# Two-scale attention and a token-choosing MLP on one core: loads in rows of 4,608 B, ranking scores transposed and counted whole, and another table of places

## The chip, the cores and the metric

The kernel runs on one core of one Trainium2 chip. The metric is the device time of one execution in microseconds; before the change the median of three runs is 291.59 us (290.5 to 292.26).

## What is computed

Inputs are q, k and v of 8 batches, 8 heads, 576 tokens and 64 numbers, and the weights of a small MLP. The reference, cut to what matters:

```python
# per batch and head; sm_attn is softmax attention
q_d, k_d, v_d = means of q, k, v over 4 neighbouring tokens      # 144 coarse tokens
out_up    = np.repeat(sm_attn(q_d, k_d, v_d), 4, axis=2)
mask      = abs(pos[:, None] - pos[None, :]) < 4                 # a band of 7 keys
out_local = softmax(where(mask, scale * q @ k.T, -1e9)) @ v
x         = (out_up + out_local) as [batch, 576, 512]
# per batch
scores  = x @ w_gate
top_idx = the 128 tokens with the highest score
h       = maximum(x[top_idx] @ w1, 0)                            # w1: 512 x 1024
out     = x;  out[top_idx] += sigmoid(scores[top_idx])[:, None] * (h @ w2)
```

## The kernel before

The host lays the inputs out, and the kernel works through eight batches in overlapping stages. For each batch b:

- **load** (`load_qk`, `load_v`): q and k of two heads share the 128 partitions; the tile T holds, per partition, four head pairs of q and k with 576 tokens each, 18,432 B. Batch 0 comes in four loads of one head pair (4,608 B a partition), every other batch in one. `raw` holds v by its four places within a coarse token, 9,216 B a partition. `vw` holds v in windows of 64 keys, in three loads. There are two buffers T and one `raw`.
- **sums** (`pool_qk`, `load_v.add`): the means over four tokens, as sums into dT and vd, by GpSimd (for batch 0 those of q and k by VectorE). `half` is the step between.
- **coarse**: scores of the coarse tokens on TensorE (line 527, with 534 for the tokens over 128), maximum on VectorE, exponentials on ScalarE, transposes (511, 589 to 591), products with vd (601 to 623), division on VectorE into ods and odr.
- **lift**: the coarse rows are repeated four times into x, for batches 0 and 1 by matmuls (`raise_by_products`, 676 to 692, with one GpSimd step `apart`, 664), for the others by DMA copies within SBUF (`raise_by_copies`).
- **local**: banded attention in five tiles of 116 queries: mask and scores (754, 766), maximum and difference (777, 778), exponential (786), transposes (511), products (812), division (822 to 824), the sum into x (834: VectorE for batches 0 and 7, GpSimd for the rest) and the dot product with the gate (841). Then x is stored to DRAM.
- **route**: the 128 highest of 576 scores. The scores stand as 5 columns of 128 in `scp`. `rows` transposes each column, spread over 128 columns, so that every partition sees all scores (895). `compare` (908) then sets on VectorE, for tile j, where a score of tile j or later is beaten, and sums that up for tile j; `count` (919) adds on TensorE what the later tiles lost in these comparisons. `rank` joins the two, `hot` makes one-hot columns, `pick` (946) turns them into token numbers, and `gather` fetches the tokens' rows of x from DRAM.
- **moe**: `turn` (984) transposes the 128 rows, eight `up` blocks (1005 to 1007, 12 matmuls each) and eight `down` blocks (1027 to 1029, three each) are the MLP with f16 weights in high and low parts, `join` (1035) multiplies by the gate and `scatter` writes the rows back.

Each stage is cut into steps, 934 in all, each of one engine. A planner keeps lists of what is ready and hands out buffers; which ready step comes next is told by PLACES, a table of 934 numbers, one for each step, the lowest first. The instructions of each engine then stand in that order and wait in that order. All loads and stores but the gather and scatter are issued by SP, which also issues in order. The wait for a buffer, for instance the one `raw`, holds up what SP issues behind it.

In the names of the rows, `ps` is PSUM, `hid` is also the buffer in which the f32 weights land, `xe` that of the gate at the start, and `cst` the constants, which come in two loads (lines 360 and 386).

Of the kernel before, what the change touches and what calls it, by code (L numbers as in the profile page):

```python
# [11 lines left out]
F32 = mybir.dt.float32  # L12
F16 = mybir.dt.float16
BF16 = mybir.dt.bfloat16
# [66 lines left out]
"""  # L81


class Buf:


    def __init__(self, tag, line=None):
        self.tag, self.line, self.at, self.left = tag, line or tag, None, 0
        self.banks = {"pair": 2, "bank": 1}.get(tag, 0)

# [1049 lines left out]
```

## Time and profile before

| | |
|---|---|
| median of three runs | 291.59 us |
| lowest and highest | 290.5 and 292.26 us |
| the profiled execution's own time | 292.61 us |
| its span | 290.8 us |
| mean granted TensorE clock | 0.962 of full speed |
| busy: TensorE matmuls | 233.5 us (80%) |
| busy: VectorE | 216.1 us (74%) |
| busy: GpSimd | 162.8 us (56%) |
| busy: ScalarE | 127.3 us (44%) |

The profile is of one execution, and its times are of that one. A busy share is a mean over stages with different limits; the table by stage and the lists of waits say more on which engine sets the pace where. "Idle before, releaser" names what ended the wait of an instruction; "issue" stands where the trace shows nothing that the engine waited for. PE is TensorE, PEld its weight loads, DVE VectorE, ACT ScalarE, POOL GpSimd, SPq the queue of SP.

### The profile page before, as it was taken

The page shows a single profiled execution, that of the slowest core. Times are in us where ns is not written, and L with a number is a line of the kernel's source. Part 1 is how long each engine was busy: PE and PEld are TensorE (multiplying, and loading weights), DVE is VectorE, ACT ScalarE, POOL GpSimd, SP SyncE. Part 2 cuts the span into 40 slices and gives each one's busy share as a digit, 9 for nine tenths or more (in the row PEclk, how much of TensorE's full clock was granted, in tenths as well). Part 3 has the DMA queues.
Part 4 walks back from the last instruction along what each step waited for, and adds up shares of the span by engine and source line. Part 5 has one row for each costly group of instructions (what it writes and reads, how often), then busy time and mean ns, then how long its engine had stood idle before and what let it go on. Part 6 is the DMA issues. An engine that isn't in the chain of part 4 may idle for free.

```text
span 290.8 us, 12080 instructions
## 1 busy us (share of the span) xinstructions
PE 233.5 (80%) x5280; PEld 171.6 (59%) x5280; DVE 216.1 (74%) x507; ACT 127.3 (44%) x264; POOL 162.8 (56%) x177
## 2 busy tenths in 40 slices
PE   1776966498677677997789989899999899789892
PEld 0654553366446556755676658756885775657570
DVE  5986497986996969977968799688988888632121
ACT  0476475348573445256605544365333233041010
POOL 8248878369876858939696976943613302202011
PEclk9999799969999957999999999999999999999998
DMA  7999978666798999868997598786887703502000
GB/s 273 423 412 389 407 280 327 241 149 177 238 341 292 315 341 377 257 197 261 347 278 223 174 325 270 194 214 140 205 240 187 182 17 103 135 2 72 2 36 36
DMA packets 19518, 66.01 MB, mean 227 GB/s; under 512 B 3346, under 2 KB 3346, under 8 KB 17546
## 3 DMA queue, kind: packets, MB, share of 16 engines
q1 hardware_dynamic: 18186, 61.06, 64.9%
q0 software_dynamic: 1280, 4.20, 4.4%
q8 instruction: 41, 0.67, 0.9%
q14 instruction: 11, 0.09, 0.1%
HBM read 47.02 MB, written 11.73 MB: 202 GB/s over the span
## 4 chain that ended last, share of the span: by engine, by line
PE 51%; issue 14%; DVE 13%; DMA 8%; ACT 6%; SPq 3%; POOL 1%; POOLq 0%; DVEq 0%
PE ps L766 5%; PE ps L1005 5%; PE ps L812 5%; PE ps L511 4%; PE ps L1027 4%; DMA out_dram<-x 4%; PE ps L1007 4%; PE ps L1006 4%; PE ps L1029 3%; PE ps L1028 3%; PE ps L527 2%; DMA T<-in_qk_dram 2%; PE ps L609 2%; DMA hid<-in_moe_w_dram 2%; DVE t L841 2%
## 5 line engine op out<-in xcount | busy, mean ns | idle before, releaser
L834 POOL TENSOR_TENSOR x<-x,t 128x512 f32<-128x512 f32 x30 | 39.3, 1320 | 21.1 <-DVE t L824 13.3
L1005 PE MATMUL ps<-xeh,w1h 128*128 128x128 f16 x256 | 45.2, 220 | 3.5 <-DVE hid L1017 1.7
L1007 PE MATMUL ps<-xeh,w1l 128*128 128x128 f16 x256 | 45.0, 219 | 0.0
L1006 PE MATMUL ps<-xel,w1h 128*128 128x128 f16 x256 | 45.0, 219 | 0.0
L766 PE MATMUL ps<-T 64*58 64x64 f32 (+1 forms) x1280 | 28.3, 230 | 6.6 <-issue 6.5
L777 DVE TENSOR_REDUCE mx<-ps 128x16 f32<-128x1024 f32 (+1 forms) x24 | 25.0, 1042 | 10.5 <-PE ps L766 10.5
L812 PE MATMUL ps<-vw,pt 64*64 64x65 f32 x1280 | 28.1, 226 | 5.4 <-ACT ed L559 1.5
L766 PEld LDWEIGHTS ps<-T 64*58 64x58 f32 (+1 forms) x1280 | 26.9, 139 | 9.1 <-issue 8.2
L841 DVE SCALAR_TENSOR_TENSOR t<-x,ps 128x512 f32<-128x512 f32 x40 | 26.9, 684 | 7.0 <-PE ps L1007 3.9
L490 POOL TENSOR_TENSOR half<-T 128x1152 f32<-128x1152 f32 x14 | 29.5, 2106 | 3.9 <-DMA T<-in_qk_dram 3.6
L812 PEld LDWEIGHTS ps<-vw,pt 64*64 64x64 f32 x1280 | 22.9, 136 | 13.6 <-issue 4.2
L798 ACT COPY pt<-ps 128x1024 f32<-128x1024 f32 (+1 forms) x24 | 20.8, 872 | 19.3 <-PE ps L511 19.3
L824 DVE TENSOR_TENSOR t<-ps,den 128x512 f32<-128x512 f32 x40 | 27.7, 691 | 1.5
L1014 ACT ACTIVATE hid<-ps 128x512 f16<-128x512 f32 x16 | 9.6, 597 | 43.7 <-PE ps L1007 21.2
L1006 PEld LDWEIGHTS <-w1h 128*128 128x128 f16 x256 | 25.0, 98 | 4.9 <-issue 4.1
L786 ACT ACTIVATE ex<-ex 128x1024 f32<-128x1024 f32 (+1 forms) x24 | 22.0, 916 | 13.3 <-DVE ex L778 11.9
L1027 PE MATMUL ps<-w2h,hid 128*128 128x512 f16 x64 | 24.3, 380 | 4.0 <-DVE hid L1017 1.3
L527 PE MATMUL ps<-dT 64*64 64x144 f32 x256 | 14.8, 337 | 15.3 <-DVE dT L482 7.2
L961 POOL DMA_INDIRECT xe<-out_dram,idx x8 | 8.4, 1045 | 33.4 <-DVE gs L956 22.3
L1005 PEld LDWEIGHTS <-w1h 128*128 128x128 f16 x256 | 25.0, 98 | 1.7
L778 DVE TENSOR_TENSOR ex<-ps,mx 128x1024 f32<-128x1024 f32 (+1 forms) x24 | 25.1, 1047 | 0.8
L1007 PEld LDWEIGHTS <-w1l 128*128 128x128 f16 x256 | 25.0, 98 | 0.0
(113 smaller groups left out, 533.3 us busy)
## 6 DMA issues: line engine op xcount, KB each, us to landing
T<-in_qk_dram SPq DMA_DIRECT2D x7, 2304.0 KB
raw<-in_vp_dram SPq DMA_DIRECT2D x8, 1152.0 KB
vw<-in_vw_dram SPq DMA_DIRECT2D x16, 520.0 KB
out_dram<-x SPq DMA_DIRECT2D x14, 480.0 KB
x<-ods SPq DMA_DIRECT2D x48, 120.0 KB
hid<-in_moe_w_dram SPq DMA_DIRECT2D x8, 512.0 KB
T<-in_qk_dram SPq DMA_DIRECT2D x4, 576.0 KB
vw<-in_vw_dram SPq DMA_DIRECT2D x8, 260.0 KB
```

The costliest lines, as they stand in the source:

```text
L490: pool.tensor_tensor(out=hv.at, in0=e2[..., 0], in1=e2[..., 1], op=ALU.add)
L766: pe.matmul(s.at[64 * e : 64 * e + qn, a, c : c + KW], lhsT=T.at[64 * a : 64 * a + 64, hp, 0, q0s[blk] : q0s[blk] + qn], rhs=T.at[64 * a : ...
L777: dve.tensor_reduce(out=mx.at[:, :, :ng], in_=sv, axis=AX.X, op=ALU.max)
L778: dve.tensor_tensor(out=ex.at[:, :ng, :].rearrange("p g (a c) -> p a g c", a=2), in0=sv, in1=mx.at[:, :, :ng].unsqueeze(3).broadcast_to([P ...
L812: pe.matmul(o.at[64 * e : 64 * e + 64, a, D1 * hp : D1 * (hp + 1)], lhsT=pt.at[64 * a : 64 * a + 64, e, HP * n + hp, :], rhs=vl.at[64 * a ...
L824: dve.tensor_tensor(out=t.at.rearrange("p (g a d) -> p a g d", a=2, d=D), in0=ov[:, :, :, 0:D], in1=den.at.unsqueeze(3).broadcast_to([P, 2 ...
L834: (dve if last else pool).tensor_tensor(out=x.at[:, j], in0=x.at[:, j], in1=t.at, op=ALU.add)
L841: dve.scalar_tensor_tensor(out=t.at, in0=x.at[:, j], scalar=1.0, in1=wg, op0=ALU.mult, op1=ALU.mult, accum_out=sc.at[:, j : j + 1],)
L1005: pe.matmul(o, lhsT=w1h[:, c, fs], rhs=xeh.at[:, c, :], start=c == 0, stop=False)
L1006: pe.matmul(o, lhsT=w1h[:, c, fs], rhs=xel.at[:, c, :], start=False, stop=False)
L1007: pe.matmul(o, lhsT=w1l[:, c, fs], rhs=xeh.at[:, c, :], start=False, stop=c == NC - 1)
L1027: pe.matmul(py.at, lhsT=hid.at[:, 0, f, :], rhs=w2h[:, f, :], start=f == 0, stop=False)
```

## The change

It has three parts. First, the host lays q and k out with the head pair outermost, and v in two halves by place, so that a load that had one row of 18,432 B (q and k) or 9,216 B (v) for a partition now has four or two rows of 4,608 B for it; the tiles in SBUF and the number of loads stay. Second, `rows` transposes each column of scores in one piece of 128 partitions in place of two of 64, so that the rows stand one after the other, and `count` counts a tile's 128 tokens with one matmul in place of two; `compare` sees the same numbers in another layout. Third, PLACES has other numbers, so that the order of the steps changes on every engine. The planner's cost of `rows` goes from 390 to 550.

```diff
 PLACES = """
-    0 1 10 23 18 68 73 2 3 4 5 6 25 32 8 9 7 12 67 75 15 62 208 79 112 151 156 193 211 214 238 249 221 245 253 267 288
+    0 1 10 12 18 49 50 2 3 4 5 6 25 33 7 8 9 11 37 46 15 52 59 51 88 173 63 98 185 177 207 248 190 231 244 256 287 317
...
-    B, _, HP, _, S = qk.shape
+    B, HP, _, _, S = qk.shape
...
-    first = cpool.tile([P, 2, NT, 64], F32, name="first")
+    first = cpool.tile([P, NT * P], F32, name="first")
...
-    slots("beat", 3, [P, 2, NT, 64], BF16)
+    slots("beat", 3, [P, NT, P], BF16)
...
-                sp.dma_start(out=T.at[:, n * u : n * (u + 1)], in_=qk[b][:, n * u : n * (u + 1)])
+                sp.dma_start(out=T.at[:, n * u : n * (u + 1)], in_=qk[b, n * u : n * (u + 1)].rearrange("h p n s -> p h n s"))
...
-            "SP", 0, lambda: sp.dma_start(out=raw.at, in_=vp[b]), (), (raw,), pref("load", b, 0.35),
+            "SP", 0, lambda: sp.dma_start(
+            out=raw.at.rearrange("p (r s) h d -> p r (s h d)", r=2), in_=vp[b].rearrange("r p s h d -> p r (s h d)"),
+        ), (), (raw,), pref("load", b, 0.35),
...
+            sbf = sb.at.rearrange("p a (j u) -> p (a j) u", u=P)
             for j in range(NT):
-                for e in range(2):
-                    lo, hi = 64 * e, 64 * e + 64
-                    pe.transpose(
-                        sb.at[:, e, 64 * j : 64 * j + 64], scp.at[lo:hi, j : j + 1].broadcast_to([64, P]),
-                        ident[lo:hi, lo:hi],
-                    )
+                pe.transpose(sbf[:, j], scp.at[:, j : j + 1].broadcast_to([P, P]), ident)
...
-        step("PE", 390, rows, (scp, "cst", "cbf"), (sb, q), pr, 170)
+        step("PE", 550, rows, (scp, "cst", "cbf"), (sb, q), pr, 170)
...
                 for k in range(j + 1, NT):
-                    for e in range(2):
-                        pe.matmul(
-                            q.at[64 * e : 64 * e + 64, k : k + 1], lhsT=beat.at[:, e, k - j], rhs=ones, start=False,
-                            stop=j == NT - 2, skip_group_check=True,
-                        )
+                    pe.matmul(
+                        q.at[:, k : k + 1], lhsT=beat.at[:, k - j], rhs=ones, start=False,
+                        stop=j == NT - 2, skip_group_check=True,
+                    )
...
-    qk = np.stack([q, k]).reshape(2, B, hp, 2, S, D).transpose(1, 3, 5, 2, 0, 4)
-    qk = np.ascontiguousarray(qk).reshape(B, 2 * D, hp, 2, S)
+    qk = np.stack([q, k]).reshape(2, B, hp, 2, S, D).transpose(1, 2, 3, 5, 0, 4)
+    qk = np.ascontiguousarray(qk).reshape(B, hp, 2 * D, 2, S)
...
-    return qk, vw.reshape(B, 2 * KW, NBLK, hp, D + 1), np.concatenate([main, rest], axis=3)
+    return qk, vw.reshape(B, 2 * KW, NBLK, hp, D + 1), np.concatenate([main, rest], axis=3).reshape(B, P, 2, 2, H + 1, D).transpose(0, 2, 1, 3, 4, 5)
```

Where the table moves the first loads on SP, the order before, from the load of batch 0's v (raw) on; T0 and T1 are the two buffers for q and k, hid those for the weights, xe the gate:

```order
L441 DMA raw0_86<-in_vp_dram 128x2304
L468 DMA vw20_85<-in_vw_dram 128x520
L468 DMA vw00_83<-in_vw_dram 128x1040
L468 DMA vw10_84<-in_vw_dram 128x1040
L433 DMA T1_78<-in_qk_dram 128x4608
L404 DMA hid0_154<-in_moe_w1_dram 128x1024
L404 DMA hid1_155<-in_moe_w1_dram 128x1024
L386 DMA cst_67<-in_const_dram 128x768
L383 DMA xe0_147<-in_moe_w_gate_dram 128x512
L441 DMA raw0_86<-in_vp_dram 128x2304
L433 DMA T0_77<-in_qk_dram 128x4608
```

And the same stretch of SP now:

```order
L441 DMA raw0_86<-in_vp_dram 128x2x1152
L470 DMA vw00_83<-in_vw_dram 128x1040
L470 DMA vw10_84<-in_vw_dram 128x1040
L470 DMA vw20_85<-in_vw_dram 128x520
L404 DMA hid0_154<-in_moe_w1_dram 128x1024
L383 DMA xe0_147<-in_moe_w_gate_dram 128x512
L404 DMA hid1_155<-in_moe_w1_dram 128x1024
L386 DMA cst_67<-in_const_dram 128x768
L433 DMA T1_78<-in_qk_dram 128x4x1152
L441 DMA raw0_86<-in_vp_dram 128x2x1152
L433 DMA T0_77<-in_qk_dram 128x4x1152
```

Batch 1's q and k (T1) moved behind two weight loads, the gate and the second constants; batch 1's v and batch 2's q and k follow as before.

GpSimd waits for these loads. Before, from batch 0's last small steps (erx) on; `half` and `dT` are batch 1's sums, `first` the constant of the comparisons:

```order
L574 COPY erx0_94<-ed0_91 128x128
L490 TENSOR_TENSOR half0_79<-T1_78 128x1152
L494 TENSOR_TENSOR dT0_80<-half0_79 128x576
L490 TENSOR_TENSOR half0_79<-T1_78 128x1152
L494 TENSOR_TENSOR dT0_80<-half0_79 128x576
L388 COPY first_71<-cst_67 128x2x64
L448 TENSOR_TENSOR vd1_88<-raw0_86 128x9x64
```

And now:

```order
L576 COPY erx0_94<-ed0_91 128x128
L388 COPY first_71<-cst_67 128x128
L666 TENSOR_TENSOR t2_118<-odr0_103,cst_67 128x512
L492 TENSOR_TENSOR half0_79<-T1_78 128x1152
L496 TENSOR_TENSOR dT0_80<-half0_79 128x576
L450 TENSOR_TENSOR vd1_88<-raw0_86 128x9x64
L452 TENSOR_TENSOR vd1_88<-vd1_88,raw0_86 128x9x64 x2
L492 TENSOR_TENSOR half0_79<-T1_78 128x1152
```

The copy of `first` and batch 0's `apart` (t2) moved ahead of batch 1's sums, and batch 1's sums of v in between their two halves.

On TensorE, the ranking of batch 0 before (scp are the scores, beat the comparisons), with the steps that stand between:

```order
L895 MATMUL ps2_65<-cst_67,scp0_128 128x64 x10
L900 LDWEIGHTS identb_68
L900 MATMUL ps3_66<-off_70,identb_68 128x5
L601 MATMUL ps1_64<-vd1_88,ptr1_100 32x65 x8
L609 MATMUL ps1_64<-vd1_88,pt0_113 64x65 x16
L616 MATMUL ps1_64<-vd1_88,ptr1_100 64x65 x4
L623 MATMUL ps1_64<-vr1_90,ptr1_100 64x260 x4
L919 LDWEIGHTS beat0_136
L919 MATMUL ps3_66<-ones_72,beat0_136 64x1
```

And now, where the first count has four such pairs, and had eight:

```order
L896 MATMUL ps0_63<-cst_67,scp0_128 128x128 x5
L898 LDWEIGHTS identb_68
L898 MATMUL ps3_66<-off_70,identb_68 128x5
L814 MATMUL ps1_64<-vw10_84,pt2_115 64x65 x16
...
L768 MATMUL ps2_65<-T0_77 58x64 x32
L916 LDWEIGHTS beat0_136
L916 MATMUL ps3_66<-ones_72,beat0_136 128x1
```

Ten transposes became five of twice the width, the counting matmuls have 128 rows of output in place of 64, and other steps stand between the transposes and the count.

## Rows read from the trace of the kernel before

**Rows 1.** Page, part 1: busy us, share of the span, instructions of each engine

```profile
PE 233.5 (80%) x5280; PEld 171.6 (59%) x5280; DVE 216.1 (74%) x507; ACT 127.3 (44%) x264; POOL 162.8 (56%) x177
```

**Rows 2.** By stage: stretch, us, PE PEld DVE ACT POOL busy, clock, DMA, GB/s

```profile
7.30:30.00 22.70, 15.42 (x476) 12.74 (x480) 17.79 (x31) 13.55 (x25) 12.47 (x10) 0.99 1.00 406
...
100.00:146.30 46.30, 36.53 (x891) 27.34 (x891) 39.14 (x88) 24.37 (x52) 32.09 (x36) 0.89 0.90 299
146.30:205.00 58.70, 54.15 (x1260) 39.58 (x1261) 47.02 (x140) 28.48 (x67) 41.17 (x45) 1.00 0.80 224
205.00:252.60 47.60, 44.05 (x937) 33.57 (x937) 40.20 (x107) 15.01 (x29) 13.59 (x24) 1.00 0.61 159
```

**Rows 3.** TensorE's waits: line, waited for, us in total, times, longest

```profile
PE ps L766 <- issue: 6.5, 8, 2.2
...
PE ps L527 <- issue: 2.8, 1, 2.8
...
PE ps L812 <- issue: 1.4, 2, 1.1
```

**Rows 4.** Chain of waits from 26 us: start us, us, what

```profile
26.13 0.60 PE ps L527 x13
26.73 2.83 issue
```

**Rows 5.** TensorE in order of time: start us, us, group, idle before

```profile
48.42 0.28 PE L766 MATMUL ps<-T 64*58 64x64 f32 x4 [2.25 <-issue]
...
146.34 0.26 PE L601 MATMUL ps<-vd,ptr 128*32 128x65 f32 x4 [2.29 <-issue]
...
187.41 0.28 PE L766 MATMUL ps<-T 64*58 64x64 f32 x4 [0.98 <-issue]
```

**Rows 6.** Page, DMA: all packets by size; instruction queues' packets and MB

```profile
DMA packets 19518, 66.01 MB, mean 227 GB/s; under 512 B 3346, under 2 KB 3346, under 8 KB 17546
...
q8 instruction: 41, 0.67, 0.9%
q14 instruction: 11, 0.09, 0.1%
```

**Rows 7.** Work in two stalls of TensorE, columns as in rows 2

```profile
26.73:29.56 2.83, 0.00 (x0) 0.00 (x0) 2.47 (x5) 0.85 (x2) 2.75 (x2) 1.00 1.08 453
...
186.43:187.41 0.98, 0.00 (x1) 0.01 (x1) 0.34 (x1) 0.95 (x3) 0.91 (x1) 1.00 0.37 102
```

**Rows 8.** SP's issues of q and k: start us, us

```profile
17.05 0.37 SPq L433 DMA_DIRECT2D T<-in_qk_dram  x1
...
42.72 0.33 SPq L433 DMA_DIRECT2D T<-in_qk_dram  x1
...
136.25 0.34 SPq L433 DMA_DIRECT2D T<-in_qk_dram  x1
```

**Rows 9.** Loads of q and k, and after a stall, as rows 2

```profile
3.00:8.50 5.50, 1.29 (x16) 0.80 (x20) 4.61 (x8) 0.00 (x0) 3.40 (x5) 1.00 1.00 392
16.50:20.00 3.50, 1.87 (x80) 1.59 (x80) 2.72 (x7) 3.47 (x9) 1.11 (x3) 1.00 0.99 427
30.00:33.40 3.40, 3.40 (x77) 2.39 (x69) 1.00 (x1) 0.49 (x2) 3.24 (x5) 0.54 1.01 434
```

**Rows 10.** VectorE in order of time

```profile
32.40 1.22 DVE L777 TENSOR_REDUCE mx<-ps 128x16 f32<-128x1024 f32 x1 [3.17 <-PE ps L766]
```

**Rows 11.** TensorE in order of time: ranking, and whole transposes (L984)

```profile
208.39 0.50 PE L895 MATMUL ps<-cst,scp 64*128 64x64 f32 x10
...
139.02 0.66 PE L984 MATMUL ps<-cst,xe 128*128 128x128 f32 x4
...
212.53 0.39 PE L919 MATMUL ps<-ones,beat 128*64 128x1 bf16 x14
...
217.83 0.28 PE L946 MATMUL ps<-va,oh 128*128 128x5 bf16 x5
```

**Rows 12.** GpSimd in order of time

```profile
22.64 2.10 POOL L490 TENSOR_TENSOR half<-T 128x1152 f32<-128x1152 f32 x1 [2.30 <-DMA T<-in_qk_dram]
```

More of the change, by code (lines that the diff above doesn't have):

```diff
@@ L387, in tile_multires_attention_moe @@
     step("ACT", 600, lambda: act.copy(wg, wgs.at), (wgs,), ("wg",), -0.3)
-    step("POOL", 420, lambda: pool.tensor_copy(first[:, :, 0], const("first").rearrange("p (e u) -> p e u", e=2)), ("cst2", "zero"), ("first",), -0.3)
+    step("POOL", 420, lambda: pool.tensor_copy(first[:, :P], const("first")), ("cst2", "zero"), ("first",), -0.3)
     def load_weights():
@@ L906, in compare @@
             def compare(j=j, beat=beat):
-                flat = lambda t: t.rearrange("p e j u -> p e (j u)")
+                sr = sb.at.rearrange("p a u -> p (a u)")
                 dve.scalar_tensor_tensor(
-                    out=flat(beat.at[:, :, : NT - j]), in0=sb.at[:, :, 64 * j : 64 * NT],
-                    scalar=scp.at[:, j : j + 1], in1=flat(first[:, :, : NT - j]), op0=ALU.subtract,
+                    out=beat.at[:, : NT - j].rearrange("p j u -> p (j u)"), in0=sr[:, P * j : P * NT],
+                    scalar=scp.at[:, j : j + 1], in1=first[:, : P * (NT - j)], op0=ALU.subtract,
                     op1=ALU.is_gt, accum_out=acc.at[:, j : j + 1],
```

64 rows, old and new, of the table PLACES are left out of this document.

## The prediction

> **What bounds the kernel now.** I read the page's engine summary first, then the work by stage, then TensorE's waits, then the DMA queue. TensorE is the busiest engine [rows 1], but which engine sets the pace depends on the stage [rows 2]. From 146.3 us to 252.6 us TensorE is busy 54.15 + 44.05 of 106.3 us, so there it is nearly full and every TensorE microsecond added or taken shows in the end. Before that it is not full: 36.53 of 46.30 us in the last early stage, with VectorE at 39.14, and at the start the DMA engines are busy for the whole stage (share 1.00, 406 GB/s). So early in the program the time is set by a chain of loads, VectorE and TensorE, and what TensorE loses there by waiting is not made up, since its backlog of MLP matmuls is carried to the end.
>
> What TensorE waits for matters, then. Four groups of its matmuls wait for "issue", that is for nothing that the trace shows: 6.5 + 2.8 + 1.4 us [rows 3] and 2.3 us in one wait of line 601 [rows 5], 13.0 us together. The reader is to see that these are few and long: 2.83, 2.25 and 2.29 us are more than half, and each stands inside a run of equal matmuls of one step, where no data can be missing: 2.83 us after 13 matmuls of batch 1's first scores [rows 4], 2.25 and 2.29 us the same [rows 5]. A run of matmuls that stops halfway lacks its next instructions. The queue list has an instruction queue of 41 packets and 0.67 MB [rows 6], 16 KB each; TensorE has 10,560 instructions [rows 1], 258 for each such packet, VectorE, ScalarE and GpSimd together under a thousand. So I take queue 8 to be TensorE's instruction stream, which travels on the same 16 DMA engines as the data.
>
> During the 2.83 us stall the DMA engines are full (share 1.08, 453 GB/s); in the 0.98 us one they are not (0.37) [rows 7]. The queue's issues put a load of q and k ahead of each of the three long stalls: issued at 17.05 (after v of batch 1), 42.72 and 136.25 us, for stalls that end at 29.56, 48.42 and 146.34 us [rows 8]; that the load is under way in the stall I infer from issue and DMA share, since the rows show no landing. The page counts 19,518 packets, of which 19,518 - 17,546 = 1,972 are of 8 KB or more [rows 6]. Seven loads of T with one row of 18,432 B for each of 128 partitions, eight of raw with one of 9,216 B, and the 41 + 11 instruction packets make 896 + 1,024 + 52 = 1,972. So the long rows do travel as single packets, and they are the only data packets of that size.
>
> **The change, part by part.** *Packets.* The same bytes go as 7 x 512 + 8 x 256 = 5,632 packets of 4,608 B in place of 1,920 long ones. If an instruction packet waits behind a few data packets that an engine has taken in already, its wait shrinks with their size. I bound the gain from both sides by the rows: nothing, if the wait goes by bytes, and 12.0 us, if all of the 13.0 us but the 0.98 us without a large load goes [rows 3, 5]. I take half, 6.0 us: 17,546 - 3,346 = 14,200 packets of 2 to 8 KB [rows 6] are the usual company of the instruction packets, and without a long row near only stalls under 1 us are seen, but an instruction packet's own 16 KB and its landing stay. [...] What is late next is VectorE: it worked through most of the stall (2.47 of 2.83 us) [rows 7], but then waited 3.17 us for the scores that the stall delayed [rows 10], so most of the early gain stays. I give back a quarter of 6.8 us, 1.7 us. Net -5.1 us.
>
> The smaller rows load more slowly. Batch 0's q and k already load as rows of 4,608 B: 392 GB/s at a DMA share of 1.00, against 427 GB/s with rows of 18,432 B [rows 9]. A load of 2.36 MB is then 6.0 in place of 5.5 us, one of v some 0.25 us longer. Only in the first 30 us are the engines full throughout, and two loads of T and one of raw lie there: between 0 and 1.2 us, I take +0.6. [...]
>
> *Ranking scores.* For each batch ten transposes of halves become five of whole rows, and twenty counting matmuls become ten. Ten half transposes take 0.50 us; four whole ones of f32 take 0.66 us, 0.165 each, so five take up to 0.83: +0.33 us. Counting: fourteen half matmuls take 0.39 us, 28 ns each, and five matmuls against 128 columns 0.28, 56 ns each [rows 11]; ten at 56 ns cost what twenty at 28 ns do. Six of eight batches are ranked where TensorE is nearly full, 2.0 us. These averages also hold each short group's end, which the next matmuls overlap, so I take +1.3 (bounds 0 and 8 x 0.33 = 2.6). VectorE's five comparisons keep their 640 to 128 elements, and the 15 fewer matmuls and 15 fewer weight loads a batch, 240 instructions in all, are one instruction packet of 41.
>
> *The table.* The table moves every engine's work. At the start SP now issues two w1 loads, the gate and the second constants ahead of batch 1's q and k: 2 x 512 + 256 + 384 KB, 1.7 MB or 4.0 us at 427 GB/s. In the trace GpSimd waits for that load until 22.64 us [rows 12], so it gets the load about 4 us later. Against that, GpSimd now does the const copy and batch 0's `apart` in that wait, and TensorE raises batch 0's x before it comes to batch 1's scores, work that stood behind before. GpSimd's order then meets the old one at batch 2's sums. At the end the two tables agree: behind the last `pick` both leave twelve blocks of MLP matmuls, one `turn`, four blocks, and batch 7's sixteen. I take 0 for the table, between +4 and -4 us.
>
> **Sum.** -5.1 + 0.6 + 1.3 + 0 = -3.2 us. The profiled execution took 292.61 us (span 290.8), which gives 289.4; it lies 1.02 us above the median of 291.59, so the forecast is 291.59 - 3.2 = 288.4 us.
>
> **Rivals.** *The wait goes by bytes.* If an instruction packet waits until what was queued ahead of it is through, size does not matter, the 13.0 us stay, and the change doesn't do what it says. For it: the 0.98 us stall has no q and k load near. Against: the three longest all have one. The time is then 291.59 + 0.6 + 1.3 = 293.5 us. [...]
>
> *The late load decides.* If TensorE runs out of batch 0's work before batch 1's sums are there, the 4.0 us are added to the chain of loads, VectorE and TensorE at 22.64 us and nothing later gives them back: 288.4 + 4.0 = 292.4 with the fetch gain, 292.4 + 5.1 = 297.5 without, 295.0 between. It decides from the point where the work of batch 0 that now fills TensorE's wait lasts less long than the load is late. With the late load and a fetch gain under half of the forecast's it ends slower, and this case holds mostly those.
>
> [...]
>
> **How the numbers follow.** About half a percent (1.46 us) is what a measurement of this kernel tells from no change: below 290.1 is faster, above 293.1 slower. Forecast 0.48 (0.43 faster, 0.05 same); bytes 0.24 (half same, half slower); late load 0.15 (all but 0.02 slower); all stalls gone 0.13. So faster 0.56, same 0.19, slower 0.25. The range reaches from near the last case, 282.5, into the late load, 295.5; the forecast's own range, with its table term, is 284.4 to 292.4.
>
> **What would show it.** Right: the "issue" groups of TensorE sum to 6 or 7 us, no stall over 1.5 us beside a load of q and k, the clock not at half about 30 us, five transposes in about 0.8 us. Wrong: the same 13 us of "issue" at other places, or GpSimd's first wait for T over 5 us with TensorE idle behind it, or TensorE less than 0.92 busy after 146 us, which would say that the table lost the cover of the MLP matmuls.

## The result, and the profile after

The changed kernel's median is 286.84 us over six runs (281.51 to 288.32), that of the kernel before beside it 291.98 us (290.50 to 294.71): 5.1 us less, where 3.2 us had been forecast. The ratio is 0.9647, 95% interval 0.9589 to 0.9705; it leaves out runs over 1.5% above the fastest, four of the changed kernel's six, which is why it is further from 1 than the medians are. By the ratio the gain is some 10 us, three times the forecast. Two later comparisons gave 0.9890 (0.9804 to 0.9975; medians 286.21 and 290.47) and 0.9758 (0.9686 to 0.9831; 283.47 and 294.47). Faster, then, by 1 to 3.5%. The first two intervals do not touch, though the two kernels are the same, so an interval here does not hold all that differs from one comparison to the next. A ratio is good to about a per cent either way, and differences of that size between builds that were not measured side by side say little.

The lines below are of the changed kernel's first profile, span 281.0 us. First the page's engine summary [rows 1] and the packets by size [rows 6]:

```profile
PE 230.4 (82%) x5160; PEld 172.9 (62%) x5160; DVE 211.6 (75%) x507; ACT 127.9 (46%) x264; POOL 164.0 (58%) x177
...
DMA packets 23229, 66.00 MB, mean 235 GB/s; under 512 B 3346, under 2 KB 3346, under 8 KB 23178
```

The 1,920 long packets are gone: 23,229 - 23,178 = 51 packets of 8 KB and more are left, the instruction packets (40 of q8 and 11 of q14). The change does what it says. Next the work by stage, columns as in [rows 2]:

```profile
7.30:30.00 22.70, 17.00 (x387) 11.71 (x387) 16.98 (x26) 13.64 (x25) 9.50 (x9) 0.92 1.02 398
...
100.00:146.30 46.30, 38.41 (x944) 30.53 (x933) 36.77 (x88) 22.01 (x47) 32.39 (x36) 0.96 0.85 255
146.30:205.00 58.70, 54.21 (x1276) 40.83 (x1276) 50.18 (x142) 28.73 (x67) 40.79 (x43) 1.00 0.84 242
205.00:252.60 47.60, 44.67 (x913) 35.10 (x911) 40.69 (x114) 17.32 (x35) 11.52 (x22) 1.00 0.59 151
```

After 146.3 us TensorE is busy 54.21 + 44.67 of 106.3 us, 0.93, as before (0.92): the cover of MLP matmuls held. The two stages shown ahead of that hold more TensorE busy time than before (17.00 for 15.42, 38.41 for 36.53), the one between them as much (52.26 for 52.37). Now TensorE's waits, as in [rows 3]:

```profile
PE ps L814 <- issue: 7.5, 5, 2.9
PE ps L529 <- DVE dT L484: 7.3, 2, 6.4
PE ps L768 <- issue: 4.4, 5, 2.1
PE ps L591 <- DVE t L843: 2.7, 1, 2.7
PE ps L603 <- ACT ptr L596: 2.7, 1, 2.7
...
PE ps L513 <- issue: 1.5, 1, 1.5
...
PE ps L529 <- POOL dT L496: 1.0, 1, 1.0
```

All of TensorE's rows with "issue" come to 14.4 us (14.1 in the kernel before). **The stalls that the packets were to halve are all there**, at other matmuls. What shrank are TensorE's waits for the other engines and for data: 36.7 us before, 30.0 now, the sum of the other rows of that list. The two spans differ by 9.8 us: 6.4 of them lie in TensorE's waits (50.8 and 44.4 in all) and 3.1 in its busy time (233.5 and 230.4). Two waits of the kernel before; the like of the first is now the 2.7 us of L591, and the second has none:

```profile
PE ps L589 <- DVE den L822: 3.9, 1, 3.9
PE ps L527 <- POOL x L834: 3.4, 1, 3.4
```

### The profile page after: what moved, and what is told of

Read it like the earlier page. It is cut to its first block, busy times and chain, and to the rows that moved or that the text cites. A ratio compares the mean times of both kernels' runs of the same rounds, so it can differ in the third digit from the quotient of the medians.

```text
span 281.0 us, 11847 instructions
## 1 busy us (share of the span) xinstructions
PE 230.4 (82%) x5160; PEld 172.9 (62%) x5160; DVE 211.6 (75%) x507; ACT 127.9 (46%) x264; POOL 164.0 (58%) x177
## 2 busy tenths in 40 slices
DMA packets 23229, 66.00 MB, mean 235 GB/s; under 512 B 3346, under 2 KB 3346, under 8 KB 23178
## 4 chain that ended last, share of the span: by engine, by line
PE 41%; DVE 16%; issue 15%; DMA 11%; POOL 10%; ACT 6%; SPq 1%; POOLq 0%; DVEq 0%; ACTq 0%
DMA xe<-out_dram,idx 5%; PE ps L814 4%; PE ps L1002 4%; PE ps L1004 3%; PE ps L1003 3%; PE ps L1024 3%; PE ps L513 3%; PE ps L1026 3%; PE ps L1025 3%; DVE t L843 3%; DMA T<-in_qk_dram 2%; POOL half L492 2%; DMA raw<-in_vp_dram 2%; PE ps L768 2%; PE ps L611 2%
## 5 line engine op out<-in xcount | busy, mean ns | idle before, releaser
L836 POOL TENSOR_TENSOR x<-x,t 128x512 f32<-128x512 f32 x30 | 39.2, 1315 | 19.9 <-DVE t L826 12.4
L814 PE MATMUL ps<-vw,pt 64*64 64x65 f32 x1280 | 29.0, 227 | 9.0 <-issue 7.5
L814 PEld LDWEIGHTS ps<-vw,pt 64*64 64x64 f32 x1280 | 23.9, 137 | 17.1 <-issue 11.4
L768 PE MATMUL ps<-T 64*58 64x64 f32 (+1 forms) x1280 | 26.5, 228 | 4.4 <-issue 4.4
L768 PEld LDWEIGHTS ps<-T 64*58 64x58 f32 (+1 forms) x1280 | 25.5, 138 | 6.6 <-issue 5.4
L788 ACT ACTIVATE ex<-ex 128x1024 f32<-128x1024 f32 (+1 forms) x24 | 21.9, 915 | 15.3 <-DVE ex L780 15.1
L906 DVE SCALAR_TENSOR_TENSOR beat<-ps,scp,first 128x640 bf16<-128x640 f32 (+4 forms) x40 | 22.6, 613 | 5.6 <-PE ps L896 5.1
L1024 PE MATMUL ps<-w2h,hid 128*128 128x512 f16 x64 | 24.3, 380 | 1.9 <-DVE t L843 1.3
L800 ACT COPY pt<-ps 128x1024 f32<-128x1024 f32 (+1 forms) x24 | 20.9, 878 | 10.7 <-PE ps L513 10.3
L1026 PE MATMUL ps<-w2h,hid 128*128 128x512 f16 x64 | 24.2, 379 | 0.0
L1025 PE MATMUL ps<-w2l,hid 128*128 128x512 f16 x64 | 24.2, 379 | 0.0
```

Source lines behind the costliest of these rows:

```text
L768: pe.matmul(s.at[64 * e : 64 * e + qn, a, c : c + KW], lhsT=T.at[64 * a : 64 * a + 64, hp, 0, q0s[blk] : q0s[blk] + qn], rhs=T.at[64 * a : ...
L814: pe.matmul(o.at[64 * e : 64 * e + 64, a, D1 * hp : D1 * (hp + 1)], lhsT=pt.at[64 * a : 64 * a + 64, e, HP * n + hp, :], rhs=vl.at[64 * a ...
L836: (dve if last else pool).tensor_tensor(out=x.at[:, j], in0=x.at[:, j], in1=t.at, op=ALU.add)
L1024: pe.matmul(py.at, lhsT=hid.at[:, 0, f, :], rhs=w2h[:, f, :], start=f == 0, stop=False)
L1025: pe.matmul(py.at, lhsT=hid.at[:, 0, f, :], rhs=w2l[:, f, :], start=False, stop=False)
L1026: pe.matmul(py.at, lhsT=hid.at[:, 1, f, :], rhs=w2h[:, f, :], start=False, stop=f == NF - 1)
```

## The experiments

Each kernel ran beside the kernel before on its chip; "issue" and "data" are the two sums of TensorE's waits just explained, from one profile each.

**The parts, alone and in pairs.** The first part alone, on the kernel before:

```diff
-    sp.dma_start(out=T.at[:, ...], in_=qk[b][:, n * u : n * (u + 1)])
+    sp.dma_start(out=T.at[:, ...], in_=qk[b, n * u : n * (u + 1)].rearrange("h p n s -> p h n s"))
-    sp.dma_start(out=raw.at, in_=vp[b])
+    sp.dma_start(out=raw.at.rearrange(..., r=2), in_=vp[b].rearrange("r p s h d -> p r (s h d)"))
```

> The kernel before with rows of 4608 B alone; its ranking and its table stay. Theory 1, fetch waits shrink with the row (the forecast's): -4.5 us against before, ratio about 0.985, and TensorE's groups that wait for issue fall from 13.0 to 6 or 7 us. Theory 2, the gain is the table's: between 0 and +1.2 us, ratio 1.000 to 1.004, and 12 to 14 us of issue. Theory 3, the gain needs the parts together: within 1.5 us of before.

The table alone:

```diff
 PLACES = """
-    0 1 10 23 18 68 73 2 3 4 5 6 25 32
+    0 1 10 12 18 49 50 2 3 4 5 6 25 33
```

> The kernel before with the new table alone; long rows, ranking in halves. Theory 1: 0 us against before, ratio 1.000. Theory 2: -9 to -12 us, ratio 0.96 to 0.97, whatever the rows are. Theory 3: half of the gain or less, ratio 0.98 to 1.00, as the table's order was set for loads and a ranking of the other form.

The ranking alone:

```diff
-    for e in range(2):
-        pe.transpose(sb.at[:, e, 64 * j : 64 * j + 64], ...)
+    pe.transpose(sbf[:, j], scp.at[:, j : j + 1].broadcast_to([P, P]), ident)
```

> The kernel before with scores transposed and counted whole alone. By the forecast's term +1.3 us (0 to +2.6), ratio 1.0045, under theories 1 and 2. Theory 3: between -2 and +2 us, as the 240 instructions less move the places at which TensorE's instruction packets end.

Then the changed kernel with one part undone each: the first part's lines back to long rows,

```diff
-    in_=qk[b, n * u : n * (u + 1)].rearrange("h p n s -> p h n s")
+    in_=qk[b][:, n * u : n * (u + 1)]
```

> The changed kernel with the rows of 18432 and 9216 B of before: only the packets undone. Theory 1: +4.5 us against the changed kernel, so 0.98 of before. Theory 2: as the changed kernel, 0.962 to 0.968 of before, or up to 1.2 us under it. Theory 3: at least 3 us above the changed kernel, 0.975 of before or more.

the ranking back to halves,

```diff
-    pe.transpose(sbf[:, j], ...)
+    for e in range(2):
+        pe.transpose(sb.at[:, e, 64 * j : 64 * j + 64], ...)
```

> The changed kernel with scores transposed and counted in halves again: packets and table without the ranking. Parts that add up: 0.996 of before. Parts that need each other, with the ranking among them: 0.98 to 0.99; with the ranking as a bystander: as the changed kernel.

and the table back to the old one,

```diff
-    0 1 10 12 18 49 50 2 3 4 5 6 25 33
+    0 1 10 23 18 68 73 2 3 4 5 6 25 32
```

> The changed kernel with the table of before: packets and ranking without the table. Parts that add up: 0.990 of before. If the gain beyond the ranking's is the table's, now that loads and ranking are the ones it was set for: 0.988 to 0.995, and the changed kernel lies 2 to 7 us under it.

The whole change, unedited, beside the last two:

> The changed kernel once more, beside the three next ones on one chip, as the parts alone gave 0.998 (packets), 0.998 (table), 0.992 (ranking), and table with ranking 0.984. Parts that add up: 0.980 to 0.985 of before. Parts that need each other: 0.960 to 0.972, as first measured.

| kernel | median, us | before beside it | ratio (95%) | issue, us | data, us |
|---|---|---|---|---|---|
| before (profile) | | | | 14.1 | 36.7 |
| packets | 290.31 | 294.41 | 0.998 (0.990 to 1.006) | 9.7 | 33.2 |
| table | 291.12 | 294.41 | 0.998 (0.989 to 1.007) | 16.2 | 35.1 |
| ranking | 289.21 | 294.41 | 0.992 (0.984 to 1.000) | 15.9 | 34.3 |
| table, ranking | 286.43 | 294.41 | 0.984 (0.976 to 0.991) | 13.4 | 30.2 |
| packets, table | 286.49 | 290.47 | 0.986 (0.979 to 0.994) | 18.7 | 24.7 |
| packets, ranking | 286.81 | 290.47 | 0.989 (0.983 to 0.995) | 10.3 | 37.4 |
| all three | 286.21 | 290.47 | 0.989 (0.980 to 0.998) | 14.0 | 31.3 |

Packets and ranking alone are not worth what was forecast for them (-4.5 and +1.3 us), the table alone is (0). Any two give about what all three gave beside them (0.989), and less than all three gave in the first comparison (0.965). The first theory (packets, -4.5 us, ratio 0.985) falls by the packets alone, 0.998. The kernel without them does not decide it: its 0.984 is what both the first and the third theory allow. The kernel with packets alone shows that a smaller sum of stalls need not pay. Its engine summary and two of its waits, and the summary of the table alone:

```profile
PE 238.0 (83%) x5280; PEld 174.4 (61%) x5280; DVE 215.8 (75%) x507; ACT 127.5 (44%) x264; POOL 163.4 (57%) x177
...
PE ps L529 <- issue: 4.0, 2, 2.7
PE ps L768 <- issue: 2.7, 7, 0.6
...
PE 233.7 (80%) x5280; PEld 174.6 (60%) x5280; DVE 216.9 (75%) x507; ACT 127.4 (44%) x264; POOL 163.5 (56%) x177
```

With packets alone issue is 4.4 us less than before, but TensorE's busy time for the same 5,280 matmuls is 238.0 in place of 233.5 us: 4.5 us given back. The mean granted clock is lower too, 0.939 against 0.962, but that alone does not explain it: the table alone has 0.938 and 233.7 us. The second theory (the table owns all of it) falls by the table alone. What is left is the third, that parts go together, or a plain sum of small parts: those of the parts alone are 0.990, 0.996 and 0.990 for the three pairs, in the order of the table, and 0.988 for all three. Of the four kernels only packets with table lies outside its interval then (0.979 to 0.994), and that by less than the comparisons scatter. The runs do not tell these two apart.

**Rows still shorter, and the bytes taken away.** The changed kernel with rows of 1,152 B (q, k) and 2,304 B (v), and, with y=4 and v in 12 pieces, of 576 and 768 B; the host lays the inputs out to match:

```diff
-    out=T.at[:, n * u : n * (u + 1)]
+    out=T.at[:, n * u : n * (u + 1)].rearrange("p h n (y s) -> p (h n y) s", y=2)
...
-    out=raw.at.rearrange("p (r s) h d -> p r (s h d)", r=2)
+    out=raw.at.rearrange("p (r s) h d -> p r (s h d)", r=4)
```

> The changed kernel with still shorter rows: q and k in 16 rows of 1152 B for a partition, v in 4 of 2304 B; same bytes, same number of loads. If TensorE's waits for instructions shrink with the row: issue falls by a third or more from the 14 us of the changed kernel, and 2 to 4 us less. If they go by bytes: 12 to 16 us of issue, and 0 to +4 us, since more packets load more slowly.

> The changed kernel with rows of 576 B for q and k (32 for a partition) and 768 B for v (12). If TensorE's waits shrink with the row: issue at 10 us or less, and at least the gain of rows of 1152 B (3 us under the changed kernel), unless the load is slower. If they go by bytes: 12 to 16 us of issue, and the loads at the start, now in packets under a KB, run at 300 to 380 GB/s in place of 410, which costs 3 to 6 us.

And the changed kernel with most of the loads of q, k and v left out, so that 48.3 MB are moved in place of 66.0:

```diff
 def go(u=u, n=n):
+    if b > 1:
+        return sp.dma_start(out=T.at[:, 0, 0], in_=qk[b, 0, :, 0])
...
+    sp.dma_start(out=raw.at[:, 0], in_=vp[b, 0, :, 0]) if b > 1 else ...
```

> The changed kernel with most loads of q, k and v left out: from batch 2 on only one row of 2304 B for a partition is loaded in place of q and k (18432 B) and in place of v (9216 B), and the rest is computed from what stands in the buffers, so the output differs. All instructions of the engines stay. If TensorE's long waits for issue come from instruction packets that wait behind loads: after 50 us no such wait over 1 us is left (five of 1.0 to 2.9 us in the changed kernel), all issue together is at most 8 us (14 us), and the time falls by 4 us or more. If TensorE's fetch is slow by itself: 12 to 16 us of issue, waits over 1 us every 256 instructions or a multiple of it wherever the engine runs fast.

The rows of 1,152 B gave 283.12 us (ratio 0.976, 0.967 to 0.985) with 12.0 us of issue, those of 576 B 290.16 us beside 292.05 with 15.1 us of issue. By row length the issue sums are: 18,432 B 14.1, 16.2, 15.9, 13.4; 4,608 B 14.4, 14.0, 9.7, 18.7, 10.3; 1,152 B 12.0 (and 17.0, below); 576 B 15.1. The builds with 4,608 B further down lie between 9.0 and 14.6. **The sums do not follow the row.** With 576 B the start is slower too, 350 GB/s to the 398 above:

```profile
7.30:30.00 22.70, 16.66 (x384) 13.00 (x384) 16.07 (x22) 11.97 (x23) 6.62 (x8) 0.85 1.10 350
```

With the loads left out, these are all of TensorE's waits for issue, and the longest others:

```profile
PE ps L531 <- DVE dT L486: 8.7, 2, 6.6
PE ps L605 <- ACT ptr L598: 6.3, 2, 6.0
PE ps L770 <- issue: 1.8, 3, 0.9
...
PE ps L515 <- issue: 1.5, 1, 1.5
```

Issue falls from 14 to 3.3 us, the 1.5 us one being in the start, whose loads stay. The time is 275.61 us beside 292.05, 0.944, where the changed kernel's medians gave 0.985 on the same chip (286.21 to 290.47): some 12 us. So it was the loads in flight that made TensorE wait for its instructions here. What the stalls cost is less than their sum: from the changed kernel's profile on that chip to this one issue fell by 10.7 us (14.0 to 3.3), but the waits for the other engines and for data rose by 5.3 (31.3 to 36.6), so these took up about half of what the stalls left.

**The late load.** GpSimd in the changed kernel, in order of time:

```profile
26.04 1.95 POOL L666 TENSOR_TENSOR t<-odr,cst 128x512 f32<-128x512 f32 x1 [4.66 <-DVE odr L647]
27.96 2.10 POOL L492 TENSOR_TENSOR half<-T 128x1152 f32<-128x1152 f32 x1
```

Batch 1's first sum starts at 27.96 us and at 22.64 before [rows 12], and it does not wait for its load but stands behind `apart`, which waits for VectorE. So the sums were put ahead of it:

```diff
-GpSimd: apart (batch 0), half and dT (batch 1)
+GpSimd: half and dT (batch 1), apart (batch 0)
-TensorE: raising of batch 0, coarse scores of batch 1
+TensorE: coarse scores of batch 1, raising of batch 0
```

> The changed kernel with two places of its table moved: GpSimd sums the first half of batch 1's q and k ahead of batch 0's step apart, and TensorE takes batch 1's first scores ahead of batch 0's raising. If a late load of batch 1's q and k holds the start up: no change, within 0.5%, the first sum still starts at about 28 us. If GpSimd's order does (it waited 4.66 us for VectorE's odr ahead of these sums, not for the load): the first sum starts at 21 to 23 us, VectorE's wait of 3.02 us at 32 us shrinks to under 1 us, and 1 to 3 us less, ratio to the changed kernel 0.990 to 0.997.

The same with rows of 1,152 B:

```diff
+    out=T.at[:, n * u : n * (u + 1)].rearrange("p h n (y s) -> p (h n y) s", y=2)
...
+    out=raw.at.rearrange("p (r s) h d -> p r (s h d)", r=4)
```

> Both: the moved places of the run before it, and rows of 1152 B (q, k) and 2304 B (v). Short rows gave 0.976 of before beside 0.989 for the changed kernel. If that is a gain and not scatter: 0.966 to 0.976 of before, with the sums' 1 to 3 us on top. If it was scatter: as with the moved places alone.

They took 287.16 and 290.11 us beside 292.05: no gain over the changed kernel, and the 0.976 of the short rows does not come again. GpSimd of the first:

```profile
28.04 2.11 POOL L493 TENSOR_TENSOR half<-T 128x1152 f32<-128x1152 f32 x1 [5.14 <-PE ps L815]
```

It stands first now, waits 5.14 us and starts at 28.04 all the same. In the program this step reads only T, so I put the wait down to the load, whose landing no row shows, and not to the matmul named. The load is then late by some 5.4 us, as the forecast's rival had it (4.0). Then the load itself was put back:

```diff
-SP: w1, gate, w1, second constants, batch 1's q and k
+SP: batch 1's q and k, w1, gate, w1, second constants
 (and the two moves above, the sums also ahead of the copy of first)
```

> The changed kernel with the early order of before put back for one load: batch 1's q and k are issued ahead of the weights, GpSimd sums their first half ahead of the constant first and of batch 0's apart, and TensorE takes batch 1's first scores ahead of batch 0's raising. If the table's late load costs what the forecast's rival said: the first sum starts at 21 to 23 us (28 us), VectorE's and TensorE's waits of 3.0 and 1.0 us at 30 us go, and 2 to 4 us less than the changed kernel, 0.965 to 0.972 of before. If batch 0's work covers the late load: within 1.5 us of the changed kernel, 0.973 to 0.984 of before.

It gave 0.996 (0.991 to 1.002), 289.23 us beside 290.10: the gain was gone, which neither of the two expectations had. One line each of its GpSimd, ScalarE and TensorE:

```profile
22.68 2.10 POOL L493 TENSOR_TENSOR half<-T 128x1152 f32<-128x1152 f32 x1 [5.02 <-DMA T<-in_qk_dram]
...
23.86 1.06 ACT L410 ACTIVATE w1h<-hid 128x1024 f16<-128x1024 f32 x1 [7.26 <-DMA hid<-in_moe_w_dram]
...
26.25 0.66 PE L604 MATMUL ps<-vd,ptr 128*32 128x65 f32 x16 [6.08 <-ACT ptr L597]
```

The sums start 5.3 us earlier, as expected, but now the weights are late. ScalarE's step on them stands ahead of the copy `ptr` and waits 7.26 us, and TensorE stands 6.08 us behind that. In the new table the order of the loads and that of the engines belong together: with the load and the steps that use it moved back and the rest left, new waits came that were longer than the one removed. So this run does not price the late load by itself.

**Where the instruction packets end.** 32 one-column matmuls with their weight loads, 64 instructions, were put at TensorE's start, where it waits for data until 6.45 us anyway, then 128 and 192 (64 and 96 of them):

```diff
+def idle():
+    b16 = ident.bitcast(BF16)
+    for _ in range(32):
+        pe.matmul(wg[:32, :1], lhsT=b16[:, :32], rhs=b16[:, :1], start=True, stop=True)
```

> The changed kernel with 64 more instructions on TensorE (32 one-column matmuls with their weight loads) at the program's start, where TensorE waits for its first data until 6.45 us anyway; nothing else differs. They only shift the places at which its 256-instruction packets end by a quarter of one. If these places and the waits at them decide some per cent: the time differs from the changed kernel's by up to 3 us either way, and the long waits for issue stand 64 instructions earlier in the same work. If not: within 1 us of it (1 us is what the 64 instructions take, ahead of the first data).

> The same with 128 instructions, half a packet. Places decide: up to 3 us either way of the changed kernel, and another number than with 64. Places do not matter: within 1 us.

> The same with 192 instructions, three quarters of a packet. Places decide: up to 3 us either way. Places do not matter: within 1 us, or up to 1 us above it as the added instructions may end behind the first data.

The changed kernel beside them, and the kernel before with 128:

> The changed kernel beside the three on one chip. 0.985 to 0.99 of before if its second comparison (0.989) is the true one, 0.965 if the first is.

> The kernel before with 128 more instructions on TensorE at the program's start, where it waits for its first data: its packets of instructions end half a packet earlier in the work, nothing else differs. If these places are worth some per cent whatever the table is: the time differs from before by 1 to 4 us either way, ratio 0.986 to 1.014, and the longest waits for issue (2.83, 2.25 and 2.29 us in the kernel before) stand at other matmuls. If they are worth nothing: ratio 0.997 to 1.003.

| kernel | median, us | before beside it | ratio (95%) | issue, us | clock |
|---|---|---|---|---|---|
| changed | 283.47 | 294.47 | 0.976 (0.969 to 0.983) | 13.2 | 0.949 |
| changed + 64 | 285.00 | 294.47 | 0.974 (0.966 to 0.982) | 14.6 | 0.931 |
| changed + 128 | 281.98 | 294.47 | 0.968 (0.962 to 0.974) | 10.5 | 0.955 |
| changed + 192 | 284.01 | 294.47 | 0.971 (0.963 to 0.979) | 11.7 | 0.957 |
| before + 128 | 292.24 | 290.10 | 1.012 (1.005 to 1.019) | 12.4 | 0.961 |

The stall followed here moves by the 64 instructions put ahead of it. This is TensorE about it, in the changed kernel:

```profile
104.46 0.22 PE L1004 MATMUL ps<-xeh,w1l 128*128 128x128 f16 x1
104.61 0.41 PE L756 MATMUL ps<-mask,identb 64*64 64x512 bf16 x4
104.85 0.50 PE L768 MATMUL ps<-T 64*58 64x64 f32 x21
106.74 0.82 PE L768 MATMUL ps<-T 64*58 64x64 f32 x42 [1.40 <-issue]
```

and the same work with 64 instructions ahead of it (its line numbers are seven higher):

```profile
106.21 0.22 PE L1010 MATMUL ps<-xel,w1h 128*128 128x128 f16 x1
108.33 0.23 PE L1011 MATMUL ps<-xeh,w1l 128*128 128x128 f16 x1 [1.90 <-issue]
...
108.82 0.64 PE L763 MATMUL ps<-mask,identb 64*64 64x512 bf16 x4
109.25 1.92 PE L775 MATMUL ps<-T 64*58 64x64 f32 x64
```

The stall stood behind 21 matmuls of the scores; now it stands behind the 17th of the block's 24 MLP matmuls: 7 of those, 4 of the mask and 21 of the scores earlier, 32 matmuls with 32 weight loads, 64 instructions to the one. Counted from the start, the trace has 2,002 matmuls and 2,002 weight loads ahead of the stall in both kernels, and 2,002 and 2,003 ahead of one in the kernel before, 1.09 us that end at 111.34 us, in other work (L812). This place is thus a matter of the count.

What the places are worth in time is not clear. In the kernel before the ratio says 1.2% slower with the shift, but its six runs, 287.24 to 294.40 us, lie within the seventeen beside them, 286.71 to 296.83. In the changed kernel the four medians lie 3.0 us apart, and their intervals overlap. The 128 beat both kernels in the median (281.98 us), but do not clearly differ from the changed kernel's 283.47.

## Why the prediction was right or wrong

**Direction and time.** Faster was right, and the three medians (286.84, 286.21, 283.47) lie in the range. The sum, -3.2 us, came near the medians' 5.1 and 4.3 us by luck, as its largest term was wrong; of the 10 us of the first ratio it had a third. Two terms failed: the packets, which were to bring it all and brought nothing that can be told from noise, and the table, put at 0, with which TensorE's waits for the other engines fell.

**That the stalls are TensorE's instruction packets: right.** Work and stalls stand like this in the changed kernel, columns as in [rows 2]:

```profile
105.80:107.88 2.08, 0.00 (x0) 0.00 (x1) 2.08 (x7) 1.89 (x7) 0.72 (x2) 1.00 0.99 358
107.88:111.80 3.92, 3.92 (x127) 3.44 (x127) 2.89 (x6) 1.11 (x2) 2.63 (x8) 1.00 1.04 318
111.80:114.73 2.93, 0.00 (x0) 0.00 (x0) 2.44 (x2) 0.40 (x1) 2.85 (x2) 0.95 0.96 309
```

Between these two stalls TensorE does 127 + 127 = 254 instructions; the forecast had 258 for each packet of the queue. From each stall of a microsecond or more in this profile to the next, from the one that ends at 18.82 us on, it does 764, 1,524, 1,271, 254, 1,528 and 1,016, which are 3, 6, 5, 1, 6 and 4 times 254 to 255, and between the ends of two waits for issue, at 101.39 and 107.88 us, 128 + 128 = 256. In both stalls above the DMA engines are full (shares 0.99 and 0.96).

**Packets, -6.0 us: the step that failed.** "If an instruction packet waits behind a few data packets that an engine has taken in already, its wait shrinks with their size" did not hold. Issue was to fall to 6 or 7 us and was 14.4, and packets alone gave 0.998 (0.990 to 1.006) where the forecast's net -4.5 us make 0.985. The rival "the wait goes by bytes" was right that the row does not matter, though its time (293.5 us) was not: rows from 18,432 to 576 B leave the sum between 9.0 and 18.7 us without an order, and taking 17.7 of the 66.0 MB away leaves 3.3. The argument that the three longest stalls all had a load of long rows near mistook the load for its rows. What exactly an instruction packet waits for stays open: in nine of the eleven stalls of a microsecond or more in the profile before and the changed kernel's first the DMA engines are nearly full (shares 0.93 to 1.11), but two of the changed kernel's, 1.04 us that end at 76.88 us and 1.12 us that end at 152.66 us, stand at 0.74 and 0.79.

**Clock, -0.8 us.** The 6.8 us of which the forecast gives back a quarter hold 0.8 us for the granted clock. No run shows this term; in its place the runs showed a clock near half as before, at another place: 0.54 from 30.0 to 33.4 us in the kernel before [rows 9], 0.55 from 39.00 to 42.40 us in the changed kernel. The stall of TensorE ahead of that, in order of time, and the work from soon after it, columns as in [rows 2]:

```profile
38.54 0.52 PE L814 MATMUL ps<-vw,pt 64*64 64x65 f32 x20 [2.12 <-issue]
```

```profile
39.00:42.40 3.40, 3.37 (x66) 2.40 (x58) 3.23 (x8) 3.30 (x6) 3.32 (x3) 0.55 0.94 357
```

After the stall of 2.08 us that ends at 107.88 us the clock is 1.00 (above), so not every stall has such a clock behind it. What the clock costs over a whole run no comparison here isolates: with the same 5,280 matmuls TensorE's busy time was 233.5 us at a mean clock of 0.962, 238.0 at 0.939 and 233.7 at 0.938.

**Smaller rows load slower, +0.6 us.** About right, though not by the step from 427 to 392 GB/s [rows 9] that it was worked out from, 8% less: the first stage moves 398 GB/s with 4,608 B (399 with packets alone) and 406 with the long rows [rows 2], 2% less, some 0.45 of its 22.7 us.

**Ranking, +1.3 us.** As work it was nearly right, and too dear. In the nearly full stage the changed kernel has

```profile
144.39 0.71 PE L896 MATMUL ps<-cst,scp 128*128 128x128 f32 x5
147.90 0.33 PE L916 MATMUL ps<-ones,beat 128*128 128x1 bf16 x7
148.75 0.19 PE L916 MATMUL ps<-ones,beat 128*128 128x1 bf16 x2
150.87 0.18 PE L916 MATMUL ps<-ones,beat 128*128 128x1 bf16 x1
```

where five transposes were to take up to 0.83 and the ten before took 0.50 [rows 11]; the counts of the kernel before at the like place are

```profile
152.59 0.39 PE L919 MATMUL ps<-ones,beat 128*64 128x1 bf16 x14
153.69 0.23 PE L919 MATMUL ps<-ones,beat 128*64 128x1 bf16 x4
154.62 0.19 PE L919 MATMUL ps<-ones,beat 128*64 128x1 bf16 x2
```

so a batch costs 0.71 + 0.70 for 0.50 + 0.81: 0.1 us more, 0.8 for eight. Yet kernels with the ranking were 0.8% faster than those without (alone), 1.4% (beside the table), and 0.3% slower (beside the other two parts). The rows of the ranking show no work that it saves. TensorE's busy time as a whole is lower with it in all four pairs of kernels (228.4 for 233.5 us alone, 231.9 for 233.7 beside the table, 229.9 for 238.0 beside the packets, 230.4 for 235.7 beside both), and why is open. Its 240 instructions less shift where the packets end, but that this is its gain is not shown.

**Table, 0 between +4 and -4 us: the term that was mis-sized.** TensorE's waits for data are 36.7, 33.2, 34.3, 37.4 and 34.5 us in the five kernels with the old table (before, packets, ranking, both, and the shift), 35.2 in the mean, and 35.1, 30.2, 24.7, 30.0, 31.3 and 32.0 in those with the new one (table, with ranking, with packets, and the changed kernel three times), 30.6: 4.7 us less. In each of the four pairs that differ by the table alone the sum is lower with it, by 1.6 us (alone) to 8.5 us (beside the packets). In time only part of it shows: 0.2% alone, 0.9% beside the ranking, 1.2% beside the packets but on another chip, nothing beside packets and ranking. That the term was not 0 is thus shown in the waits, not in the time.

**The late load** was late, 5.4 us for 4.0, but did not decide: batch 0's raising filled TensorE's wait, of which 1.0 us is left in the list above (`dT L496`). The point that the forecast named, whether that work lasts as long, went the good way.

What stays open is the cause of the gain, that is how its 3 to 10 us divide among table, ranking and the places where instruction packets end: builds that differ in one small thing lie 1 to 3 us apart, as much as the parts, and repeated comparisons of the same two kernels differ by more (1.1 to 3.5%).

## What to carry to other kernels

A TensorE stall of 1 to 3 us inside a run of equal matmuls, at multiples of the same instruction count (here 254 to 256), is here a wait for its own instructions. To tell, put idle instructions at the program's start and see whether the stall moves by as many (here by 64 for 64). These stalls went when loads were taken away (14.0 to 3.3 us of issue) and stayed when the same bytes came in other rows (12.0 and 17.0 us with 1,152 B, 15.1 with 576 B), and about half of what they left (5.3 of 10.7 us) was taken up by waits for other engines and for data. Before a gain of a per cent is put down to an edit, repeat the comparison of the same two kernels: here it gave 3.5, 1.1 and 2.4%. And when a load moves in an order, move the steps that wait for what it passes as well: the load that came 5.4 us late behind covered work left TensorE a wait of 1.0 us, and the early one, with the weights behind it, a wait of 6.1 us.

## What the runs showed that was not expected

The same two kernels compared three times gave 3.5, 1.1 and 2.4%, the first two with intervals that do not touch. A stall stands after the same count of instructions in both kernels, 4,004 or 4,005, in other work (the scores, L768, and the products, L812). Cutting rows of 4,608 B into eight of 576 B took the loads at the start from 398 to 350 GB/s, 12% less, while 18,432 to 4,608 B cost 2% (406 to 398). And the sum of TensorE's busy time is here no constant of the work: 5,280 equal matmuls took 233.5 us at a mean clock of 0.962, 238.0 us at 0.939 and 233.7 us at 0.938.
